# Two grouped-key attention layers and two gMLP layers on one core: normalisation and division moved to GpSimd, score slots of two and two banks in nine groups, a longer ring early, and a new choice of the key tiles that VectorE takes

## The chip, the cores and the metric

The kernel runs on one core of a Trainium2 chip. The core has TensorE (PE, matrix products into PSUM), VectorE (DVE) and ScalarE (ACT), which both read PSUM, GpSimd (POOL), which works on SBUF alone here, and SyncE (SP), from whose queue every DMA of this kernel is issued. The metric is the device time of one execution in microseconds (us), smaller being better. Before the change it is 1592.44 us, the median of three runs (1591.35 to 1594.88).

## The reference, cut to what matters

Four residual blocks follow each other on 2048 tokens of width 512: attention A, gMLP B, A, B, each behind a layer norm. Attention has 32 query heads of width 16 and one key and value head. Weights and tokens are bf16.

```python
def _A_ref(x, wq, wk, wv, wo):
    q = (x @ wq).reshape(B, S, 32, 16).transpose(0, 2, 1, 3)
    k = x @ wk
    v = x @ wv
    scores = jnp.einsum('bhqd,bkd->bhqk', q, k) * 16 ** (-0.5)
    p = softmax(scores)
    o = jnp.einsum('bhqk,bkd->bhqd', p, v)
    return o.transpose(0, 2, 1, 3).reshape(B, S, 512) @ wo

def _B_ref(x, w_in, w_sp, b_sp, w_out):
    z = gelu(x @ w_in)                    # 1792 columns
    z1, z2 = z[..., :896], layernorm(z[..., 896:])
    g = einsum('ts,bsf->btf', w_sp, z2) + b_sp[None, :, None]
    return (z1 * g) @ w_out

x = x + _A_ref(layernorm(x), ...)
x = x + _B_ref(layernorm(x), ...)
# and both once more
```

## The kernel before

**Work of one layer.** The 2048 tokens are 16 tiles of 128. The queries are cut in nine chunks of two tiles (the last two of one), and each chunk with its heads in 32 groups per layer; a group holds 512 query columns for each of four rows of heads. For every group and each of the 16 key tiles PE makes four score blocks of 128x512 (line 897). The exponentials of these 4096 blocks are the bulk of the kernel.

**Two ways for a key tile.** Of most key tiles the four blocks go through `push_unit` and `push_slot`: blocks are put in a row, and taken from it three and two at a time into two slots of PSUM banks, (0,1,2) and (3,4). ACT takes the exponential of a whole slot in one instruction (line 921: 128x1536 or 128x1024) into `P_ring`, which holds 20 blocks, and PE multiplies them with the values, four at a time (line 940), summing in bank 6. The key tiles that `ON_DVE` lists for the group (234 places in all) go through `push_unit_dve`: each of the four blocks goes into a side bank (5 or 7), DVE turns it into an integer that is the bit pattern of an approximate exponential (line 974, one instruction a block), makes two shifted copies of all four (line 983, 128x2048, two instructions), and PE multiplies the three versions with weighted values (line 989). So a unit on DVE is six DVE instructions, and takes four blocks from ACT. The three versions stand in the buffer `big`, of which a ring of six places is used up to group 24 and of five from there.

**End of a group.** DVE copies bank 6 out (line 1051 or 1048), SP issues a DMA transposition (line 1010), DVE takes the reciprocal of the sixteen denominators of each row (line 1017) and multiplies by it (line 1026, two instructions a group, one where the chunk is one tile), into `o_norm`. At the end of a chunk SP transposes its tiles (line 1060), PE multiplies with `wo` (line 693 is the helper of all products that are made in four column strips, line 698 of those made in one), DVE adds to the tokens `X` (line 1074).

**Layer norms.** `ln_tiles` takes statistics on DVE (lines 796, 797), the inverse deviation on GpSimd (lines 784 and 786: an addition, then a power of -0.5), and normalises a tile on DVE (line 801). `norm_z2` does the same for the gMLP's second half (lines 1251 to 1258). The transposed tokens `xnTA` and `xo` come from the normalised ones by DMA (line 810), and at the start of a layer by PE (line 815). On GpSimd there are besides these only the products of line 1364 at the end of a layer, and memsets at the start.

**gMLP.** It is spread over the attention of the same layer: the products with `w_in` behind each chunk (`b_front`), the product with `w_sp` in two stages after tiles 6 and 12 (`mix_stage`, line 1305), the rest when the layer's attention is over (`mix_late`, lines 1359 and 1364), for layer 1 between the two layers and for layer 2 at the end. The GELUs run on ACT (lines 1207, 1230, 1242 and others).

**What sets the order.** Every operation is recorded with the tiles that it reads and writes, an assumed duration and a priority. `_Graph.schedule` then plays the program through by these durations, and writes for each engine a fixed list of instructions, with semaphore waits between engines. Each engine works through its own list in order. PSUM banks are given out in that play: slots by `slots`, the side banks by `side`; where no slot waits, a free slot bank can serve as a side bank. `filler` puts matmuls that compute nothing where PE would be idle too long (lines 716, 719 and 730). `NEAR`, `P_S` (priority of the score blocks for DVE) and `HOLD_DVE` (how long such a block is held back when a slot is due) are numbers of that play.

Of the kernel before, what the change touches and what calls it, by code (L numbers as in the profile page):

```python
# [44 lines left out]
HOLDS = 1.0  # L45

ON_DVE = ((
          (6,10,14), (6,10,14), (6,10,14), (6,10,14), (4,5,6,13), (8,9,12,14), (4,7,9,10,11), (3,6,14),
          (4,7,10,14), (4,6,8,12), (5,8,9,13), (4,6,10,12), (2,5,7,9,10), (2,8,9,11,12), (5,9,13), (3,4,5,9),
          (3,10,11,14), (2,3,5,8,14), (2,4,9,14), (8,9,12,14), (7,11,13), (2,9,13,14), (3,6,10,14), (4,5,7,13),  # L50
          (3,9,12,13), (8,11,14), (10,13), (3,6,7,13), (2,6,14), (2,4,9,14), (6,10,14), (2,4,12)
), (
          (6,10,14), (10,14), (6,10,14), (14,), (6,10,14), (2,10,14), (2,6,10), (10,14), (4,5,12,14),
          (7,8,11,12,13), (4,5,7,14), (3,12,13,14), (4,8,13), (4,6,9,14), (4,5,6,12), (3,5,8,12),
          (2,7,8,11,14), (3,9,10), (3,4,5,6,12), (7,8,9,10,13), (6,8,13,14), (6,7,9,11), (2,3,4,8,11),
          (6,13,14), (2,5,6,11), (5,7,10), (4,5,7,13), (5,11,13), (4,6,12), (2,8,9,12), (4,8,9,10), (2,3,8,10)
))


# [4 lines left out]
SLOTS_STAGE = ((12, 13, 14, 15), (10, 11, 12, 13, 14, 15), (10, 11, 12, 13, 14, 15))  # L64
FRONTS = (((0, 4, None), (4, 2, 0), (6, 2, None), (8, 4, 6), (12, 2, None), (14, 1, 12), (15, 1, 15)), ((0, 4, None), (4, 2, 0), (6, 2, None), (8, 4, 6), (12, 2, None), (14, 1, 12), (15, 1, 15)))
SHORT_RING = (24, 24)
Z2_LATE = (12, 12)

PR_FRONT = (0.5, 3.5)
WARM_US = 3.4  # L70
WARM = 0.52
WARM_END = 0.55
NEAR = 1
LEAD_PR = 4
GELU_PARTS = 1
EAGER = 4
CHAIN_ACT = 1
KEY_PR = {0: 1.2, 2: 1.7, 4: 2.2, 6: 2.4, 8: 2.7, 10: 2.9, 12: 3.2}
KEYS = (((0, 2), (2, 2), (4, 4), (8, 4), (12, 4)), ((0, 2), (2, 2), (4, 4), (8, 4), (12, 4)))
NFIRST = (4, 8)  # L80
# [2 lines left out]
SLOTS_LATE = ((0, 1, 2, 3, 4, 5, 6), (7, 12, 13, 14, 15, 6), (0, 1, 2, 3, 4, 5, 6, 7, 8, 9, 10, 11, 12, 13, 14, 15))  # L83
POOL0 = {0: (), 2: (0, 1, 2, 3, 4, 5, 6), 4: (1, 3, 5)}
POOL1 = (0, 2, 4, 6)
HOLD_DVE = (1.0, 1.0, 0.4, 1.0)
STAY = 0.3
P_S = 0.2
P_R = 0.3
P_A = 4.0  # L90
WARM_OP = 0.217
# [63 lines left out]
class _Graph:  # L155
# [67 lines left out]
    def schedule(self):  # L223
# [27 lines left out]
        warm = WARM  # L251
        slot_ops = [o for o in self.ops if o.task is not None and o.task.slot is not None and o.eng == "pe"]
        slot_at = 0
        slot_due = -1.0

        def push(t, what, x):
# [14 lines left out]
        def met(s, p):  # L271
# [8 lines left out]
            if s.nleft == 0 and (t is None or t.ops[0] is not s):  # L280
                make_ready(s)

        def banks_for(o):

            t = o.task
            if t.slot is not None:
                bs = self.slots[t.slot]
                return bs if all(bank_free[b] for b in bs) else None
            bs = [b for b in self.side if bank_free[b]]
            if not bs and slot_wait == 0:  # L290
                bs = [b for s in self.slots for b in s if bank_free[b]]
            return bs[:1] or None

        def acquire(o, bs):
# [59 lines left out]
        def filler():  # L354


            nonlocal wake
            if self.warm is None or not 0.0 <= self.warm_after.t0 < now - 0.5:
                return None
            while past and past[0][0] < now - WARM_US:  # L360
                past.pop(0)
            have = sum(x for _, x in past)
            if have >= warm * WARM_US:
                drop = next(t for i, (t, _) in enumerate(past)
                            if have - sum(x for _, x in past[:i + 1]) < warm * WARM_US)
                t = max(drop + WARM_US, now) + 0.01
                if wake < now or t < wake:
                    wake = t
                    push(t, 2, None)
                return None  # L370
            if pv_open:
                m = 0 if last_mode == 0 else 2
                o = _Op("pe", lambda e: self.zeros(e, m), WARM_OP, PE_LAT, FILLER, len(self.ops), None, None, m)
                o.deps[self.warm_after] = 1
                self.ops.append(o)
                return o
            bs = [b for b in self.side if bank_free[b]]
            if not bs and slot_wait == 0:
                bs = [b for s in self.slots for b in s if bank_free[b]]
            if pv_empty is not None:  # L380
                bs = [self.pvb]
            if not bs:
                return None
            b = bs[0]
            m = 0 if last_mode == 0 else 2
            o = _Op("pe", lambda e: self.warm(e, b, m), WARM_OP, PE_LAT, FILLER, len(self.ops), None, None, m)
            o.deps[self.warm_after] = 1
            if b == self.pvb:
                o.deps[pv_empty] = 1
                self.ops.append(o)  # L390
                return o
            for q in bank_last[b]:
                o.deps[q] = max(o.deps.get(q, 0), 0 if q.eng == "pe" else 1)
            self.ops.append(o)
            return o
# [153 lines left out]
def bass_interleave_layers__grouped_kv_mqa__mixer_gmlp__prompt_kernel(  # L549
# [17 lines left out]
    QC = 512  # L567
    NQC = S // QC
    CT = QC // P
    G = _Graph(nc, (5, 7), ((0, 1, 2), (3, 4)))  # L570
    op = G.op

    ps_all = G.es.enter_context(nc.psum_tensor("ps_all", [P, 4096], FP32))
# [17 lines left out]
    ident32 = G.sb([P, P], FP32, "ident32")  # L591
    idle = G.sb([P, 1], FP32, "idle")
    mhalf = G.sb([P, 1], FP32, "mhalf")
    X = G.sb([P, NT, D], BF16, "X")

    kT_rep = G.sb([P, 2, S], BF16, "kT_rep")
# [72 lines left out]
    def dve(fn, us, r, w, prio=5):  # L669
        return op("dve", fn, max(us - DVE_LAT, 0.06), r=r, w=w, prio=prio, lat=DVE_LAT)  # L670
# [29 lines left out]
    def side(wide):  # L700
# [5 lines left out]
    op("pool", lambda e: e.affine_select(out=ident[:], in_=ident[:], compare_op=ALU.not_equal, fill=1.0, base=0,  # L706
                                         pattern=[[-1, P]], channel_multiplier=1), 0.3, r=["ident"], w=["ident"])
    op("pool", lambda e: e.memset(mhalf[:], -0.5), 0.1, w=["mhalf"])
    op("pool", lambda e: e.memset(zeros[:], 0.0), 0.2, w=["zeros"])
    G.warm_after = op("pool", lambda e: e.memset(ones[:], 1.0), 0.2, w=["ones"])  # L710
    G.pvb = PVB
# [79 lines left out]
    def ln_tiles(t0, n, xT, keys, per_tile, prio=5):  # L791
# [6 lines left out]
        rstd("1", ve1, rs1, mv1, t0 % CT, n, per_tile, prio)  # L798
        for t in ts:
            i = t % CT  # L800
            dve(lambda e, i=i, t=t: e.tensor_scalar(xn[:, i, :], X[:, t, :], mv1[:, i, 0:1], rs1[:, i:i + 1],
                                                    op0=ALU.subtract, op1=ALU.mult), 0.4,
                [("X", t), ("mv1", i), ("rs1", i)], [("xn", i)], prio)
        t = t0
        while t < t0 + n:
            m = 1 if per_tile else min(2, t0 + n - t)
# [69 lines left out]
        return gi // 2 % NQ, gi % 2  # L876

    main = {"blocks": [], "i": 0, "s": 0, "pv": [], "last": None}
    SLOTS = ((0, 3), (3, 2))

    def push_unit(u):

        main["pv"].append([u, 4])
        for j in range(4):
            main["blocks"].append((u, j))
        while len(main["blocks"]) >= SLOTS[main["i"] % 2][1]:
            push_slot(SLOTS[main["i"] % 2][1])

    def flush_units():
        if main["blocks"]:  # L890
# [9 lines left out]
    def push_slot(n):  # L900
        blocks = main["blocks"][:n]
        del main["blocks"][:n]
        i = main["i"] % 2
        main["i"] += 1
        b0 = SLOTS[i][0]
        s0 = main["s"] % NPR
        main["s"] += SLOTS[i][1]
        tk = _Task(i)

        def pe_s(e):  # L910
# [86 lines left out]
    def finish_group(gi):  # L997
# [15 lines left out]
        def src():  # L1013
            if not isinstance(tk, _Task):
                return ot[:, par, :, :].rearrange("p b (j r) -> p b j r", j=4)
            return bank16(tk.bank)[:, 0:CT * P].rearrange("p (b j r) -> p b j r", b=CT, j=4)
        dve(lambda e: e.reciprocal(rden[:], src()[:, :, :, DH]), 0.26, [tk], ["rden"], pr)
        a = g % 2
        cs = [g // 2 * m + u for u in range(m)]
        if n == 1:  # L1020
# [1 line left out]
        else:  # L1022
            parts = [(u * n, n, o_norm[:, i0:i0 + n, c * P:(c + 1) * P].rearrange(
                "p b (j a d) -> p a b j d", j=4, a=2)[:, a], [c]) for u, c in enumerate(cs)]
        for b0, nb, dst, of in parts:
            dve(lambda e, b0=b0, nb=nb, dst=dst: e.tensor_tensor(
                dst, src()[:, b0:b0 + nb, :, 0:DH], rden[:, b0:b0 + nb, :, None].to_broadcast([P, nb, 4, DH]),
                ALU.mult), 0.15 + 0.07 * nb, [tk, "rden"],
                [("on", c, a, i) for c in of for i in range(i0, i0 + n)], pr)
# [57 lines left out]
    def attn_first(t0, n):  # L1087

        for gi in range(NFIRST[now["layer"]]):
            have = sum(GROUPS[gi][:2])  # L1090
            if have > t0 + n:
                continue
# [16 lines left out]
    def attn_rest():  # L1109
        phr["base"] = 0  # L1110
        for gi in range(NFIRST[now["layer"]], len(GROUPS)):
            now["group"] = gi
            on_dve = ON_DVE[now["layer"]][gi]
            phr["ring"] = NRING if gi < SHORT_RING[now["layer"]] else 5
            for kt in range(NT):
                u = (q_of(gi), kt, kt == 0, kt == NT - 1, lambda gi=gi: group_done(gi, False),
                     kt >= NT - 1 - NEAR)
                if kt in on_dve:
                    push_unit_dve(u)
                else:  # L1120
                    push_unit(u)
# [124 lines left out]
    def norm_z2(t0, n, fine, pr):  # L1246
# [8 lines left out]
        rstd("2", ve2, rs2, mv2, t0 % CT, n, fine, pr)  # L1255
        for t in ts:
            i = t % CT
            dve(lambda e, i=i, t=t: e.tensor_scalar(z2n[:, t, :], z2n[:, t, :], mv2[:, i, 0:1], rs2[:, i:i + 1],
                                                    op0=ALU.subtract, op1=ALU.mult), 0.45,
                Z2(t) + [("mv2", i), ("rs2", i)], Z2(t), pr)  # L1260

    gs = {"n": 0}

# [222 lines left out]
```

## Time and profile before

| | |
|---|---|
| median of three runs | 1592.44 us |
| the profiled execution, its own time | 1594.17 us |
| its span | 1592.4 us |
| granted TensorE clock, mean | 0.995 |
| GpSimd busy | 88.5 us in 138 instructions |
| DMA queues, share of 16 engines | 25.5% |
| first exponential / last exponential of line 921 starts | 15.25 us / about 1514 us |
| tail after attention | 1516 to 1592.4 us, ACT busy 18.9 us of it |

A page of the profile gives busy times of the engines, their busy share in 40 slices of the span, the chain of waits that ended last, and groups of equal instructions with the mean duration of one. Two instructions of one engine can overlap at their ends, so that the distance from one start to the next is less than the duration: two instructions of line 974 of 684 ns each take 1.20 us together. Busy time counts such overlaps once.

### The profile page before, as it was taken

To read this page: it belongs to the slowest core of one execution; us is meant where nothing else is said; L and a number is where in the kernel's file an instruction comes from. 1 tells how busy PE (TensorE), PEld (TensorE's weight loads), DVE (VectorE), ACT (ScalarE), POOL (GpSimd) and SP (SyncE) were. 2 spreads that over 40 slices of the span, in tenths; PEclk is the share of its full clock that TensorE was granted. 3 is DMA by queue.
4 is the path that set the end of the run, shared out by engine and by line. 5 is a ranking of instruction groups with operands and counts; after the bars stand their busy time and mean duration, and the time that the engine had idled before them with its cause. 6 is when DMAs were issued, how large, how long until landed. Compare 5 with 4: busy or idle time off the path is not lost.

```text
span 1592.4 us, 41272 instructions
## 1 busy us (share of the span) xinstructions
PE 1499.7 (94%) x18283; PEld 492.4 (31%) x18311; DVE 1370.3 (86%) x2482; ACT 1501.3 (94%) x1312; POOL 88.5 (6%) x138
## 2 busy tenths in 40 slices
PE   8989899999999999999899989999999999999989
PEld 3222222232333333333422222323223323323344
DVE  7888889999998888896788789999899998988876
ACT  6999999999999999999699999999999999999950
POOL 2000000000000000000311000000000000000033
PEclk8999999999999999999999999999999999999999
DMA  4500010101021342645321021101121114245483
GB/s 104 130 15 11 8 28 8 16 10 41 21 48 51 90 108 68 170 98 157 116 81 34 15 52 34 22 8 19 47 64 28 22 51 107 48 124 134 114 240 131
DMA packets 188562, 106.38 MB, mean 67 GB/s; under 512 B 151264, under 2 KB 160096, under 8 KB 188384
## 3 DMA queue, kind: packets, MB, share of 16 engines
q1 hardware_dynamic: 188384, 103.75, 25.5%
q8 instruction: 143, 2.34, 0.6%
q14 instruction: 35, 0.29, 0.1%
HBM read 36.34 MB, written 31.46 MB: 43 GB/s over the span
## 4 chain that ended last, share of the span: by engine, by line
ACT 76%; PE 17%; DVE 4%; DMA 1%; issue 1%; POOL 0%; SPq 0%; DVEq 0%
ACT P_ring L921 74%; PE ps_all L693 5%; PE ps_all L897 4%; PE ps_all L698 4%; PE ps_all L940 2%; ACT z2n L1207 1%; PE ps_all L989 1%; DVE big L974 0%; DMA gp_scratch<-big 0%; DVE st L796 0%; DVE X L1074 0%; DVE st L1251 0%; DVE big L1359 0%; ACT L921 0%; DMA big<-gp_scratch 0%
## 5 line engine op out<-in xcount | busy, mean ns | idle before, releaser
L921 ACT ACTIVATE P_ring<-ps_all 128x1024 bf16<-128x1024 f32 (+1 forms) x1265 | 1433.6, 1371 | 22.0 <-PE ps_all L897 21.2
L974 DVE TENSOR_SCALAR big<-ps_all 128x512 int16<-128x512 f32 x936 | 617.7, 685 | 108.0 <-PE ps_all L897 102.7
L897 PE MATMUL ps_all<-qT,kT_rep 32*128 32x512 bf16 x4096 | 592.7, 385 | 68.2 <-ACT P_ring L921 51.6
L897 PEld LDWEIGHTS ps_all<-qT,kT_rep 32*128 32x128 bf16 x4096 | 150.3, 91 | 580.8 <-ACT P_ring L921 483.2
L983 DVE TENSOR_SCALAR big<-big 128x2048 int16<-128x2048 int16 x468 | 309.5, 683 | 3.2 <-PE ps_all L989 0.8
L940 PE MATMUL ps_all<-P_ring,V_aug 128*32 128x512 bf16 x3160 | 295.8, 387 | 2.3 <-DVE z2n L1038 0.7
L989 PE MATMUL ps_all<-big,V_ph 128*32 128x512 bf16 x2808 | 241.5, 384 | 2.1 <-DVE big L983 1.3
L940 PEld LDWEIGHTS ps_all<-P_ring,V_aug 128*32 128x32 bf16 x3160 | 75.0, 94 | 152.9 <-issue 130.3
L989 PEld LDWEIGHTS ps_all<-big,V_ph 128*32 128x32 bf16 x2808 | 66.4, 95 | 95.2 <-issue 50.1
L693 PE MATMUL ps_all<-xnTA,z2n 128*32 128x512 bf16 x1344 | 93.9, 381 | 0.0
L784 POOL TENSOR_SCALAR ve<-mv 128x1 f32<-128x1 f32 (+2 forms) x44 | 14.1, 321 | 1423.1 <-DVE mv L797 1194.8
L730 PE MATMUL ps_all<-ones,zeros 128*32 128x512 bf16 x864 | 70.5, 387 | 0.0
L693 PE MATMUL ps_all<-w_in_r,xo 128*32 128x448 bf16 x960 | 61.5, 354 | 0.0
L1074 DVE TENSOR_TENSOR X<-ps_all,X 128x512 bf16<-128x512 f32 x64 | 43.8, 685 | 18.5 <-PE ps_all L698 15.5
L693 PE MATMUL ps_all<-xo,w_in_r 128*32 128x256 bf16 (+1 forms) x1120 | 56.4, 317 | 1.0 <-DVE z1c L1197 0.5
L698 PE MATMUL ps_all<-w_out_r,z1c 128*128 128x512 bf16 x213 | 53.3, 381 | 1.1 <-issue 0.6
L1305 DVE TENSOR_TENSOR big<-ps_all,bsp 128x512 f32<-128x512 f32 x56 | 38.3, 684 | 14.4 <-PE ps_all L693 14.2
L693 PE MATMUL ps_all<-z2n 128*32 128x512 bf16 x672 | 49.1, 382 | 0.2 <-DVE big L974 0.2
L693 PE MATMUL ps_all<-z1c,z2n 128*32 128x512 bf16 x672 | 48.7, 382 | 0.0
L1305 DVE TENSOR_TENSOR big<-ps_all,big 128x512 f32<-128x512 f32 x56 | 37.9, 682 | 11.6 <-PE ps_all L693 11.4
L796 DVE BATCH_NORM_STATS2 st<-X 128x6 f32<-128x512 bf16 x64 | 43.4, 686 | 2.5 <-DMA X<-in_A_x_dram 1.8
L1359 DVE TENSOR_TENSOR big<-ps_all,big 128x512 f32<-128x512 f32 (+1 forms) x56 | 34.7, 647 | 9.5 <-PE ps_all L698 5.3
(96 smaller groups left out, 930.9 us busy)
## 6 DMA issues: line engine op xcount, KB each, us to landing
gp_scratch<-big SPq DMA_DIRECT2D x112, 256.0 KB, 2.2
big<-gp_scratch SPq DMA_DIRECT2D x105, 256.0 KB, 3.0
out_dram<-X SPq DMA_DIRECT2D x16, 128.0 KB, 1.7
w_in_r<-in_B_w_in_dram SPq DMA_DIRECT2D x1, 1792.0 KB, 9.3
big<-gp_scratch SPq DMA_DIRECT2D x14, 128.0 KB, 2.3
X<-in_A_x_dram SPq DMA_DIRECT2D x3, 512.0 KB, 6.5
bsp<-in_B_b_sp_dram SPq DMA_DIRECT2D x8, 128.0 KB, 3.6
ot<-oT SPq DMA_TRANSPOSE x62, 2.4
```

What stands on the lines that cost most here:

```text
L693: ins = e.matmul(out_[32 * j:32 * j + 32, :], lhs[:, 32 * j:32 * j + 32], rhs, tile_position=(0, 32 * j), start=start, stop=stop)
L698: return e.matmul(out_, lhs, rhs, start=start, stop=stop)
L730: ins = e.matmul(bank32(PVB)[32 * j:32 * j + 32, :], zeros[:, 0:32], mv, tile_position=(0, 32 * j), start=False, stop=False)
L796: dve(lambda e, i=i, t=t: e.bn_stats(st1[:, i, :], X[:, t, :]), 0.66, [("X", t)], [("st1", i)], prio)
L897: return e.matmul(out, kT_rep[32 * j:32 * j + 32, a, u[1] * P:(u[1] + 1) * P], qT[32 * j:32 * j + 32, q, :], tile_position=(32 * j, 0), st ...
L921: return e.activation(P_ring[:, s0:s0 + n, :], bank32(b0, n).rearrange("p (k q) -> p k q", k=n), ACTF.Exp, scale=E_SCALE)
L940: ins = e.matmul(bank32(PVB)[32 * j:32 * j + 32, :], V_aug[:, kt, :], P_ring[:, s, :], tile_position=(0, 32 * j), start=first, stop=last)
L974: o = dve(lambda e, box=box, tk=tk: e.tensor_scalar(ph16[:, tiles[0], heads["of"][box[0]] * QC:(heads["of"][box[0]] + 1) * QC], bank32(tk. ...
L983: dve(lambda e, a=a: e.tensor_scalar(ph16[:, tiles[a], :], ph16[:, tiles[0], :], float(PH_A[a]), None, op0=ALU.add), 0.69, base, BIG(tiles ...
L989: ins = e.matmul(bank32(PVB)[32 * j:32 * j + 32, :], V_ph[:, a, kt, :], big[:, tiles[a], j * QC:(j + 1) * QC], tile_position=(0, 32 * j), ...
L1074: dve(lambda e: e.tensor_tensor(X[:, t, :], bank32(tk.bank), X[:, t, :], ALU.add), 0.69, [tk, ("X", t)], [("X", t)], prio)
L1305: dve(lambda e, part=part, tk=tk: e.tensor_tensor(part, bank32(tk.bank), part if st else bsp[:], ALU.add), 0.69, [tk] + ([] if st else ["b ...
```

## The change

1. **GpSimd takes three kinds of DVE work.** `POOL_XN`: the normalising of tokens (line 801), but for the first four tiles of layer 1, for the first chunk of layer 2 and for the last chunk's part of the chain between layers. `POOL_Z2`: that of z2 (line 1258), for 24 of 32 tiles. `POOL_ON`: the division at a group's end, for 62 of 64 groups, where the reciprocal becomes a power of -1 with a tensor of minus ones (`mone`), over 128x16, and the products follow.
2. **Slots.** A third slot, (0,1), is there beside (0,1,2) and (3,4). In nine groups (five of layer 1, four of layer 2, the bits of `NARROW`) the slots alternate (0,1) and (3,4), two blocks each. Bank 2 can then serve as a side bank. The place in `P_ring` starts again at 0 where a slot would not fit.
3. **Ring.** `EARLY_RING`: in the groups below 12 the ring of `big` has eight places.
4. **Places.** `ON_DVE` is another table: 248 places, 128 in layer 1 and 120 in layer 2 (before: 119 and 115). Groups 4 to 7 of layer 1 have 5, 5, 5 and 6 (before: 4, 4, 5 and 3).
5. **Numbers of the order.** `NEAR` 1 to 0, `HOLD_DVE[0]` 1.0 to 0.6, `P_S` 0.2 to 0.6. The lists of all engines are made anew.

```diff
 ON_DVE = ((
-          (6,10,14), (6,10,14), (6,10,14), (6,10,14), (4,5,6,13), (8,9,12,14), (4,7,9,10,11), (3,6,14),
...
+          (6,10,14), (6,10,14), (6,10,14), (6,10,14), (2,4,7,12,14), (2,4,7,8,10), (2,5,9,10,12),
+          (4,5,6,9,10,12), (6,11,12,14), (2,5,10,11,14), (5,10,11,12,13), (7,8,11,13), (4,5,6,10),
...
+EARLY_RING = (12, 12)
-NEAR = 1
+NEAR = 0
+NARROW = (8407808, 84426752)
+POOL_ON = 1
+POOL_XN = 1
+POOL_Z2 = 1
-HOLD_DVE = (1.0, 1.0, 0.4, 1.0)
+HOLD_DVE = (0.6, 1.0, 0.4, 1.0)
-P_S = 0.2
+P_S = 0.6
...
+        def narrow():
+
+            while lead_slots and lead_slots[0] < slot_at:
+                lead_slots.pop(0)
+            return bool(lead_slots) and slot_ops[lead_slots[0]].task.slot == 2
...
             bs = [b for b in self.side if bank_free[b]]
+            if not bs and bank_free[2] and narrow():
+                bs = [2]
...
-    G = _Graph(nc, (5, 7), ((0, 1, 2), (3, 4)))
+    G = _Graph(nc, (5, 7), ((0, 1, 2), (3, 4), (0, 1)))
...
-            dve(lambda e, i=i, t=t: e.tensor_scalar(xn[:, i, :], X[:, t, :], mv1[:, i, 0:1], rs1[:, i:i + 1],
-                                                    op0=ALU.subtract, op1=ALU.mult), 0.4,
-                [("X", t), ("mv1", i), ("rs1", i)], [("xn", i)], prio)
+            on_pool = POOL_XN and not G.chain and (now["layer"] or t0 >= CT or xT is xo)
+            op("pool" if on_pool else "dve", lambda e, i=i, t=t: e.tensor_scalar(
+                xn[:, i, :], X[:, t, :], mv1[:, i, 0:1], rs1[:, i:i + 1], op0=ALU.subtract, op1=ALU.mult),
+               0.9 if on_pool else 0.4 - DVE_LAT, r=[("X", t), ("mv1", i), ("rs1", i)], w=[("xn", i)], prio=prio,
+               lat=0.0 if on_pool else DVE_LAT)
...
-    SLOTS = ((0, 3), (3, 2))
+
+    def next_slot():
+
+        if main["i"] % 2:
+            return 1, 3, 2
+        return (2, 0, 2) if NARROW[now["layer"]] >> now["gi"] & 1 else (0, 0, 3)
...
-        s0 = main["s"] % NPR
-        main["s"] += SLOTS[i][1]
+        if main["s"] + n > NPR:
+            main["s"] = 0
+        s0 = main["s"]
+        main["s"] += n
...
-        dve(lambda e: e.reciprocal(rden[:], src()[:, :, :, DH]), 0.26, [tk], ["rden"], pr)
+        on_pool = POOL_ON and not G.chain
+        if on_pool:
+            op("pool", lambda e: e.tensor_tensor(rden[:], src()[:, :, :, DH], mone[:, :, None].to_broadcast([P, CT, 4]),
+                                                 ALU.pow), 0.9, r=[tk, "mone"], w=["rden"], prio=pr)
+        else:
+            dve(lambda e: e.reciprocal(rden[:], src()[:, :, :, DH]), 0.26, [tk], ["rden"], pr)
...
+            if on_pool:
+                op("pool", lambda e, b0=b0, nb=nb, dst=dst: e.tensor_tensor(
+                    dst, src()[:, b0:b0 + nb, :, 0:DH], rden[:, b0:b0 + nb, :, None].to_broadcast([P, nb, 4, DH]),
+                    ALU.mult), 0.25 + 0.14 * nb, r=[tk, "rden"], w=[("on", c, a, i) for c in of for i in range(i0, i0 + n)],
+                   prio=pr)
+                continue
...
-            phr["ring"] = NRING if gi < SHORT_RING[now["layer"]] else 5
+            phr["ring"] = 8 if gi < EARLY_RING[now["layer"]] else NRING if gi < SHORT_RING[now["layer"]] else 5
...
-            dve(lambda e, i=i, t=t: e.tensor_scalar(z2n[:, t, :], z2n[:, t, :], mv2[:, i, 0:1], rs2[:, i:i + 1],
-                                                    op0=ALU.subtract, op1=ALU.mult), 0.45,
-                Z2(t) + [("mv2", i), ("rs2", i)], Z2(t), pr)
+            on_pool = POOL_Z2 and not fine and pr != 0.6
+            op("pool" if on_pool else "dve", lambda e, i=i, t=t: e.tensor_scalar(
+                z2n[:, t, :], z2n[:, t, :], mv2[:, i, 0:1], rs2[:, i:i + 1], op0=ALU.subtract, op1=ALU.mult),
+               1.5 if on_pool else 0.45 - DVE_LAT, r=Z2(t) + [("mv2", i), ("rs2", i)], w=Z2(t), prio=pr,
+               lat=0.0 if on_pool else DVE_LAT)
```

The instructions of the two built programs differ by these counts:

| engine | instruction | before | after |
|---|---|---|---|
| ACT | exponential 128x1536 (line 921) | 631 | 534 |
| ACT | exponential 128x1024 (line 921) | 633 | 751 |
| ACT | exponential 128x512 (line 921) | 1 | 0 |
| DVE | line 974, 128x512 | 936 | 992 |
| DVE | line 983, 128x2048 | 468 | 496 |
| DVE, then GpSimd | reciprocal / power 128x16 | 62 | 62 |
| DVE, then GpSimd | division, 128x128 / 128x256 | 112 / 6 | 112 / 6 |
| DVE, then GpSimd | tokens normalised, 128x512 | 64 on DVE | 8 on DVE, 56 on GpSimd |
| DVE, then GpSimd | z2 normalised, 128x896 | 32 on DVE | 8 on DVE, 24 on GpSimd |
| PE | line 940 / line 989 | 3160 / 2808 | 3104 / 2976 |
| PE | fillers (lines 716, 719, 730) | 1243 | 853 |

## The prediction

> **What bounds the kernel now.** I read the page's busy times and slices first, then the chain of waits, then the groups by form, then the waits of DVE, and last single stretches of the timeline.
>
> ```profile
> PE 1499.7 (94%) x18283; PEld 492.4 (31%) x18311; DVE 1370.3 (86%) x2482; ACT 1501.3 (94%) x1312; POOL 88.5 (6%) x138
> DVE  7888889999998888896788789999899998988876
> ACT  6999999999999999999699999999999999999950
> ```
>
> ACT is at nine tenths or more in 36 of 40 slices; it is short of work only at the start, between the layers and in the tail. PE's 94% hold 1243 fillers, so PE has room. The chain of waits (first its shares, then single pieces: start us, us, what) says the same:
>
> ```profile
> ACT 76%; PE 17%; DVE 4%; DMA 1%; issue 1%; POOL 0%; SPq 0%; DVEq 0%
> 51.88 291.64 ACT P_ring L921 x258
> 1375.66 1.20 DVE big L974 x2
> 1378.58 1.20 DVE big L983 x2
> ```
>
> In the first long piece 258 exponentials, 129 of each width, follow each other in 291.64 us: 2.26 us a pair of five blocks. The two last lines give DVE's real price: 0.60 us from start to start where the duration is 0.684, that is 0.084 less. The groups by form (mean ns after the comma):
>
> ```profile
> L921 ACT ACTIVATE P_ring<-ps_all 128x1536 bf16<-128x1536 f32 x631 | 998.9, 1583 | 7.5 <-PE ps_all L897 6.7
> L921 ACT ACTIVATE P_ring<-ps_all 128x1024 bf16<-128x1024 f32 x633 | 735.2, 1162 | 14.5 <-PE ps_all L897 14.5
> ```
>
> A block more is 1583 - 1162 = 421 ns. With 2.26 us for five blocks in two instructions, what an instruction costs by itself is (2.26 - 5 x 0.421) / 2 = 0.08 us. In 1592.4 us these instructions wait 22.0 us in all: ACT is packed, and the time falls by what its queue loses, as long as it stays packed.
>
> **ACT's queue.** 14 units move to DVE: 56 blocks x 0.421 = -23.6 us. The program has 1285 exponentials in place of 1265, since the nine narrow groups cut finer: 20 x 0.08 = +1.6. Sum **-22.0 us**. The GELUs on ACT are the same.
>
> **DVE's queue.** Added: 56 of line 974 and 28 of line 983, 84 x 0.60 = +50.4 us. Removed, each at its mean less 0.084, from these rows:
>
> ```profile
> L974 DVE TENSOR_SCALAR big<-ps_all 128x512 int16<-128x512 f32 x936 | 617.7, 685 | 108.0 <-PE ps_all L897 102.7
> L983 DVE TENSOR_SCALAR big<-big 128x2048 int16<-128x2048 int16 x468 | 309.5, 683 | 3.2 <-PE ps_all L989 0.8
> L1026 DVE TENSOR_TENSOR o_norm<-ot,rden 128x128 bf16<-128x128 bf16 x112 | 28.8, 284 | 0.4
> L801 DVE TENSOR_SCALAR xn<-X,mv,rs 128x512 bf16<-128x512 bf16 x64 | 26.9, 448 | 6.9 <-POOL rs L786 6.7
> L1017 DVE RECIPROCAL rden<-ot 128x16 f32<-128x16 bf16 x62 | 15.1, 244 | 0.2 <-DMA ot<-oT 0.2
> L1258 DVE TENSOR_SCALAR z2n<-z2n,mv,rs 128x896 bf16<-128x896 bf16 x32 | 14.9, 502 | 1.9 <-POOL rs L786 1.9
> ```
>
> 62 x 0.160 + 112 x 0.200 + 6 x 0.334 (the 128x256 form, 418 ns) + 56 x 0.364 + 24 x 0.418 = 9.9 + 22.4 + 2.0 + 20.4 + 10.0 = -64.7 us. Net -14 us: DVE as a whole gets a little lighter, and its 102.7 us of waiting for score blocks show that it has room on average. But not everywhere: counting instructions between the ends of groups in the built order, and pricing them as above, groups 5 to 9 of layer 1 have 97 us of ACT and 96 us of DVE work (before: 107 and 85). Nearly half of ACT's gain lies there, with DVE at 99%. Elsewhere DVE is near 0.89 of ACT.
>
> **GpSimd's queue.** Nothing in the trace shows these operations at these sizes. The nearest rows:
>
> ```profile
> L1364 POOL TENSOR_TENSOR z1c<-big,z1c 128x512 bf16<-128x512 f32 x25 | 32.7, 1318 | 59.7 <-DVE big L1359 59.7
> L786 POOL TENSOR_TENSOR rs<-ve,mhalf 128x4 f32<-128x4 f32 x14 | 14.7, 1049 | 1.2
> L786 POOL TENSOR_TENSOR rs<-ve,mhalf 128x1 f32<-128x1 f32 x20 | 11.6, 578 | 1.7
> L1364 POOL TENSOR_TENSOR z1c<-big,z1c 128x256 bf16<-128x256 f32 x7 | 4.5, 672 | 4.2 <-DVE big L1359 4.2
> ```
>
> The power: 0.157 us a column from 1 to 4 columns, so 16 columns are 0.578 + 15 x 0.157 = 2.93 us; the low end is 0.58 (no more than one column). I take 2.93. The division: 2.52 ns a column from 256 to 512, so 0.35 us for 128, 0.67 at the high end. Tokens, one tensor input: between 0.53 (the memset of 128x512, 527 ns) and 1.32; I take 0.9. z2, 896 columns: 0.8 (from the 128x1536 memset, 1379 ns) to 2.3; I take 1.5. Sum 62 x 2.93 + 112 x 0.35 + 6 x 0.67 + 56 x 0.9 + 24 x 1.5 = 182 + 39 + 4 + 50 + 36 = 311 us (low 120, high 390), on an engine that is busy 88.5 us. It has room; what counts is who waits for it. Behind a late power stand the two divisions, then at a chunk's end SP's transposition and PE's product with `wo`. In the built order the first such product stands at least 13.4 us of ACT work behind the last value product of the chunk. The chain needs 0.69 (line 1051) + 2.4 (DMA to landing) + 2.93 + 2 x 0.35 + 2 x 0.68 (each division once behind a line 983) + 1.24 (SP's first issue) + 2.5 (landing) = 11.8 us. It is covered, by 1.6 us. The normalised tokens: first `w_in` product at least 8.1 us behind the last PE result that its chain needs (before: 6.7), which covers the +0.5 us of the slower tile. SP's next transposition (line 1010) newly waits for GpSimd's division of two groups earlier, some 40 us before: nothing. DVE's statistics of line 797 and 1253 newly wait for GpSimd's normalising of the tile that used the place before, tens of us earlier: nothing. These cost nothing on my sum; without the cover, rival 2.
>
> **GpSimd against DVE.** The timeline shows what a neighbour costs (POOL and DVE lines of two stretches):
>
> ```profile
> 787.60 1.16 POOL L1364 TENSOR_TENSOR z1c<-big,z1c 128x512 bf16<-128x512 f32 x1
> 787.66 1.24 DVE L801 TENSOR_SCALAR xn<-X,mv,rs 128x512 bf16<-128x512 bf16 x1 [0.43 <-POOL rs L786]
> ```
> ```profile
> 1000.94 1.09 POOL L786 TENSOR_TENSOR rs<-ve,mhalf 128x4 f32<-128x4 f32 x1
> 1001.32 0.68 DVE L983 TENSOR_SCALAR big<-big 128x2048 int16<-128x2048 int16 x1
> ```
>
> The SBUF-to-SBUF instruction of DVE that starts behind GpSimd's product lasts 1.24 us, until 0.14 us after the product's end, where one without a neighbour takes 0.41 us. Line 983 beside the power keeps its 0.68. So I count GpSimd's products and normalisings as blocking (130 us of the 311), not its powers. Line 983 starts 496 times; 130 of some 1580 us is 8%, so 41 of them wait, for half of a GpSimd operation and the tail, 0.4 us: 16 us of DVE time, 0.25 us a group. Lines that read PSUM kept 0.68 beside GpSimd throughout. What of it reaches ACT: in groups 5 to 9 all of it, 1.3 us, and since DVE there has no room for any wait for a score block, some 4% of 96 us more, 4 us; in the other groups, with 2 us of room each, a fifth of the rest, 3 us. Sum **+8 us** (bounds: 0, if ACT stays as packed as now; 40, if half a microsecond a group and the early groups run at DVE's 10% idle of now).
>
> The Trainium skill (SBUF — State Buffer, Who interferes with whom) says that DVE's two-port instructions and any GpSimd operation exclude each other for the whole instruction, whoever is second. By that rule the powers would block too, which is rival 3; the row at 1001.32 disagrees, for a power of four columns.
>
> **The rest.** The longer ring frees line 983's next unit earlier in groups 4 to 11 and is what lets five units stand in a group; its places 6 and 7 are next written by line 1305, which starts after group 11: no wait. The restart of `P_ring` leaves a place or two unused at a wrap, of 20. PE: 112 value products more, 390 fillers fewer: hidden, as fillers are what is left over; if the clock fell for want of them, PEclk would leave 9. Start, layer boundary and tail: the first chunk of layer 2 keeps DVE, later chunks normalise on GpSimd behind its own line 1364 products, where DVE already waited for those (787.66). 0 us, bounds -2 and +4.
>
> **Sum.** -22 + 8 = -14: the span goes from 1592.4 to 1578.4, the profiled execution's 1594.17 to 1580.2. The median shown is 1.7 under that execution, so the forecast is **1578 us**.
>
> **Rivals.** (1) *ACT stays as packed as now*: -22, 1570 us. For it: 22.0 us of idle on line 921 in the whole run. Against it: groups 5 to 9. (2) *GpSimd is late at the ends of chunks and PE waits in order*: 16 ends at 0.5 to 1 us are 8 to 16 us on top, 1586 to 1594 us. For it: only 1.6 us of cover. Against it: DMA slack is often larger than the least. (3) *The power holds DVE off as well*: 311 us of GpSimd time block; 496 x 311/1580 = 98 starts of line 983 wait, 1.05 us on average (half of 2.93 for most), 103 us of DVE in place of 16, 1.6 us a group, of which the room of 2 us swallows half: 1578 + 43 = 1621 us, slower. It decides from 0.34 us a group (22/64) that reaches ACT. For it: xn beside line 1364; against it: three line 983 beside powers, all at 0.68 to 0.70. (4) *It does nothing*: another engine sets ACT's pace, 1592 us; against it the packed queue.
>
> **Chances.** Forecast 0.52 (its own range 1572 to 1586), rival 1 0.17, rival 2 0.15, rival 3 and milder forms of it 0.13, rival 4 0.03. A measurement here can tell about 0.2%, 3.2 us, from no change. Faster by more than that: 0.52 + 0.17 + half of rival 2 = 0.77; within: 0.06; slower: 0.17. The range 1567 to 1598 takes in rivals 1, 2 and 4, and leaves out 2 in 10.
>
> **What would show it.** Line 921: 534 and 751 instructions, its idle still under 35 us; a pair of narrow slots 2 x 0.92 us. Line 983's mean 0.70 to 0.72, not over 0.75. The power near 2.9 us. The idle of line 897 behind DVE lines up by a few us, most before 220 us. ACT's slices 9 as before. I am wrong if ACT's idle grows by more than 20 us, or if PE's waits for `wo` products show GpSimd behind them.

## The result, and the profile after

The changed kernel takes 1634.16 us (median of four runs, 1630.43 to 1634.77) against 1591.89 us before: ratio 1.0258 [1.0237, 1.0279]. By the ratio it is 41 us slower (the medians lie 42 us apart), where 14 us faster was forecast. The profiled execution took 1630.43 us; its span is 1628.5 us. Line numbers have moved: the exponential is line 946 now (921 before), scores 921 (897), products in strips 709 (693), DVE's copies 1008 (983), DVE's integers 999 (974), the value products 965 (940) and 1014 (989), other products 714 (698), the stages of `w_sp` 1344 (1305), tokens 819 (801), z2 1296 (1258), the aggregates of their statistics 814 (797) and 1290 (1253); the power and the divisions on GpSimd are 1044 and 1057, its products at a layer's end 1403 (1364).

The page after: busy times, ACT's busy share and the granted clock in 40 slices, and the shares of the chain of waits.

```profile
PE 1526.4 (94%) x18033; PEld 491.4 (30%) x18033; DVE 1373.7 (84%) x2306; ACT 1484.0 (91%) x1332; POOL 541.4 (33%) x399
...
ACT  5999999989999997999699899999799999969960
...
PEclk9999999989999998999999999999799999979999
...
ACT 60%; PE 21%; POOL 9%; DVE 6%; issue 2%; DMA 1%; SPq 0%; POOLq 0%; DVEq 0%
```

ACT lost its packed row: slices 8, 15, 28 and 35 (counted from 0) fall to 7 or 8, or to 6 in slice 35, and in the same slices the clock is below 9 (slice 22 falls to 8 with the clock at 9). GpSimd is on the chain for 9% of the span, where it had 0%. The groups of ACT and GpSimd by form (busy us, mean ns of one, idle before):

```profile
L946 ACT ACTIVATE P_ring<-ps_all 128x1536 bf16<-128x1536 f32 x534 | 830.2, 1555 | 44.1 <-PE ps_all L921 43.3
L946 ACT ACTIVATE P_ring<-ps_all 128x1024 bf16<-128x1024 f32 x751 | 806.8, 1128 | 36.0 <-PE ps_all L921 35.5
L1044 POOL TENSOR_TENSOR rden<-ot,mone 128x16 f32<-128x16 bf16 x62 | 187.6, 3026 | 697.5 <-DMA ot<-oT 697.3
L819 POOL TENSOR_SCALAR xn<-X,mv,rs 128x512 bf16<-128x512 bf16 x56 | 127.5, 2286 | 1.8
L1296 POOL TENSOR_SCALAR z2n<-z2n,mv,rs 128x896 bf16<-128x896 bf16 x24 | 85.4, 3569 | 0.7
```

In front of the exponentials ACT idles 80.1 us where it idled 22.0, nearly all of it for scores. On the page their busy time is 1416.3 us, 17.3 less than before: so -17 + 58 = +41 us on this line, more than the 36 us by which the span grew. The normalisings on GpSimd take 2.29 us a tile of tokens and 3.57 us a tile of z2; the plan assumes 0.9 and 1.5. Who waits for them (the waits of PE, then of DVE: us, times, longest):

```profile
PE ps_all L921 <- ACT P_ring L946: 31.8, 110, 1.0
PE ps_all L709 <- POOL z2n L1296: 15.9, 5, 7.0
PE ps_all L921 <- DVE big L999: 6.5, 19, 2.2
PE ps_all L1014 <- DVE big L1008: 5.6, 4, 3.4
```
```profile
DVE mv L1290 <- POOL z2n L1296: 12.5, 6, 3.6
DVE mv L814 <- POOL xn L819: 11.3, 8, 1.9
```

None of these waits on GpSimd is in the profile before. The worst place, first GpSimd and PE on the timeline, then the same stretch by windows (its length, the busy time of PE, PEld, DVE, ACT and POOL with the number of instructions, the clock, then DMA):

```profile
629.49 14.72 POOL L1296 TENSOR_SCALAR z2n<-z2n,mv,rs 128x896 bf16<-128x896 bf16 x4
...
644.26 1.05 PE L709 MATMUL ps_all<-xnTA,z2n 128*32 128x512 bf16 x8 [7.00 <-POOL z2n L1296]
```
```profile
627.00:637.00 10.00, 7.68 (x83) 2.17 (x83) 9.49 (x15) 9.12 (x8) 9.66 (x5) 1.00 0.01 2
637.00:644.00 7.00, 0.26 (x8) 0.00 (x0) 0.73 (x2) 0.14 (x1) 7.00 (x2) 0.62 0.00 0
644.00:651.00 7.00, 6.74 (x68) 1.74 (x68) 3.27 (x5) 3.86 (x4) 0.21 (x1) 0.65 0.20 59
651.00:660.00 9.00, 9.00 (x130) 2.71 (x122) 6.83 (x11) 9.00 (x9) 3.69 (x3) 1.00 0.49 142
```

PE stands in front of a `w_sp` product whose z2 tile is not there. Everything behind it on PE's list waits, the score blocks for ACT too: in these 7 us ACT is busy 0.14 us and DVE 0.73. Then the clock is at 0.65 for 7 us more and ACT gets half its work, with PE busy 6.74 of 7.00 us. So one late batch is followed by two losses: the wait, and a stretch of slow clock behind it. Over the whole run, counted record by record between the first and the last exponential, ACT idles 78.4 us where it idled 20.9. Of these 57.5 us more, 20 fall where PE stands still, 28 where PE is busy at a clock of 0.5, and 10 where PE is busy at the full clock. This says when ACT idled, not what the slow clock alone costs.

### The profile page after: what moved, and what is told of

Same layout as the page of the kernel before. It is cut to its first block, busy times and chain, and to the rows that moved or that the text cites. A ratio compares the mean times of both kernels' runs of the same rounds, so it can differ in the third digit from the quotient of the medians.

```text
span 1628.5 us, 40947 instructions
## 1 busy us (share of the span) xinstructions
PE 1526.4 (94%) x18033; PEld 491.4 (30%) x18033; DVE 1373.7 (84%) x2306; ACT 1484.0 (91%) x1332; POOL 541.4 (33%) x399
## 4 chain that ended last, share of the span: by engine, by line
ACT 60%; PE 21%; POOL 9%; DVE 6%; issue 2%; DMA 1%; SPq 0%; POOLq 0%; DVEq 0%
ACT P_ring L946 59%; PE ps_all L709 6%; PE ps_all L921 6%; POOL z2n L1296 5%; PE ps_all L714 4%; PE ps_all L965 3%; PE ps_all L1014 2%; POOL xn L819 2%; DVE big L999 1%; POOL rs L803 1%; ACT z2n L1244 1%; DVE st L813 1%; POOL rden L1044 1%; DVE st L1288 1%; DVE big L1008 0%
## 5 line engine op out<-in xcount | busy, mean ns | idle before, releaser
L946 ACT ACTIVATE P_ring<-ps_all 128x1024 bf16<-128x1024 f32 (+1 forms) x1285 | 1416.3, 1305 | 80.1 <-PE ps_all L921 78.8
L999 DVE TENSOR_SCALAR big<-ps_all 128x512 int16<-128x512 f32 x992 | 653.4, 685 | 102.9 <-PE ps_all L921 97.6
L921 PE MATMUL ps_all<-qT,kT_rep 32*128 32x512 bf16 x4096 | 615.7, 391 | 51.1 <-ACT P_ring L946 31.8
L1044 POOL TENSOR_TENSOR rden<-ot,mone 128x16 f32<-128x16 bf16 x62 | 187.6, 3026 | 697.5 <-DMA ot<-oT 697.3
L1008 DVE TENSOR_SCALAR big<-big 128x2048 int16<-128x2048 int16 x496 | 341.3, 707 | 6.0 <-PE ps_all L1014 2.7
L921 PEld LDWEIGHTS ps_all<-qT,kT_rep 32*128 32x128 bf16 x4096 | 155.9, 91 | 584.4 <-ACT P_ring L946 446.1
L1014 PE MATMUL ps_all<-big,V_ph 128*32 128x512 bf16 x2976 | 263.1, 390 | 6.4 <-DVE big L1008 5.6
L819 POOL TENSOR_SCALAR xn<-X,mv,rs 128x512 bf16<-128x512 bf16 x56 | 127.5, 2286 | 1.8
L1296 POOL TENSOR_SCALAR z2n<-z2n,mv,rs 128x896 bf16<-128x896 bf16 x24 | 85.4, 3569 | 0.7
L1057 POOL TENSOR_TENSOR o_norm<-ot,rden 128x128 bf16<-128x128 bf16 (+1 forms) x118 | 52.3, 463 | 4.7
```

The lines of the kernel that those rows point to most:

```text
L819: op("pool" if on_pool else "dve", lambda e, i=i, t=t: e.tensor_scalar(xn[:, i, :], X[:, t, :], mv1[:, i, 0:1], rs1[:, i:i + 1], op0=ALU.s ...
L921: return e.matmul(out, kT_rep[32 * j:32 * j + 32, a, u[1] * P:(u[1] + 1) * P], qT[32 * j:32 * j + 32, q, :], tile_position=(32 * j, 0), st ...
L946: return e.activation(P_ring[:, s0:s0 + n, :], bank32(b0, n).rearrange("p (k q) -> p k q", k=n), ACTF.Exp, scale=E_SCALE)
L999: o = dve(lambda e, box=box, tk=tk: e.tensor_scalar(ph16[:, tiles[0], heads["of"][box[0]] * QC:(heads["of"][box[0]] + 1) * QC], bank32(tk. ...
L1008: dve(lambda e, a=a: e.tensor_scalar(ph16[:, tiles[a], :], ph16[:, tiles[0], :], float(PH_A[a]), None, op0=ALU.add), 0.69, base, BIG(tiles ...
L1014: ins = e.matmul(bank32(PVB)[32 * j:32 * j + 32, :], V_ph[:, a, kt, :], big[:, tiles[a], j * QC:(j + 1) * QC], tile_position=(0, 32 * j), ...
```

## The experiments

**1. Is it the lateness of z2?** All lists stay as in the changed kernel; GpSimd's piece is cut until it lasts about as long as the plan assumes (340 of 896 columns, where the operation is on GpSimd).

```diff
-                z2n[:, t, :], z2n[:, t, :], mv2[:, i, 0:1], ...
+                z2n[:, t, 0:340] if on_pool else z2n[:, t, :], z2n[:, t, 0:340] if on_pool else z2n[:, t, :], ...
```

> The changed kernel with every engine's list unchanged, but GpSimd's normalising of z2 (line 1296) works on 340 of the 896 columns: 0.37 + 340 x 3.3 ns = 1.5 us, which is what the plan assumes, in place of 3.35 us. The other 556 columns stay as they are. Theory A (GpSimd is late against the plan: z2 arrives 7 us after PE's place for it, PE waits in order, its clock falls to 0.5 and ACT starves): the four places at 351, 637, 1143 and 1425 us lose their 48 us, time 1634 - 45 = 1589 us, clock 0.99. Theory B (DVE is held off at the shared port and is too full in groups 5 to 9): only the 6 us that z2 adds to line 1008 go, 1626 us. Theory C (390 fillers fewer let the clock fall by themselves): 1634 us, clock 0.97.

1593.60 us, ratio 1.0013 [0.9996, 1.0030]. 39 us of the 41 are gone with one operation's duration, at 1.72 us a tile. That is 5 us from theory A's number, while B's 1626 and C's 1634 are far off. A's clock was not reached: 0.98 to 0.99 in the ten runs, and the places where tokens are late still show a fallen clock.

**2. The tokens too, and the power too.** The first line is z2_xn_short's, on top of z2_short (160 of 512 columns, on GpSimd alone); the second is all_short's, on top of both (3 of the 16 results). What is cut away, here and in z2_short, isn't computed.

```diff
+                xn[:, i, 0:160] if on_pool else xn[:, i, :], X[:, t, 0:160] if on_pool else X[:, t, :], ...
...
+            op("pool", lambda e: e.tensor_tensor(rden[:, 0:1, 0:3], src()[:, 0:1, 0:3, DH], ...
```

> As z2_short, and GpSimd's normalising of tokens (line 819) works on 160 of 512 columns: 0.9 us, as planned, in place of 2.07 us. The other columns keep old values. Theory A: also the losses at 235, 929 and at the start go, 10 to 15 us more than z2_short: 1577 us, which is the forecast of the prediction. Theory B: 1622 us. Theory C: 1634 us.

> As z2_xn_short (every engine's list unchanged, z2 normalised on 340 of 896 columns, tokens on 160 of 512), and the power of -1 (line 1044) on 3 of 16 columns: 0.42 + 3 x 0.157 = 0.9 us, as the plan assumes, in place of 3.03 us. The other denominators are left at 1 or at old values. If the power's 2.1 us of lateness is covered, as the prediction has it: the time of z2_xn_short, 1575 us, within 3 us. If the divisions too are waited for: 1565 us or less.

z2_xn_short: 1575.32 us, 0.9895 [0.9879, 0.9911]: 19 us more where A had 10 to 15, and 2 us from A's time. all_short: 1566.57 us, 0.9846 [0.9832, 0.9861]: 8 us more, so the power's lateness was not covered. All three together: some 66 us (1.0258 - 0.9846 = 0.0412 of 1591).

Where the power costs its 8 us can be seen in z2_xn_short. Nearly all of ACT's idle time that all_short doesn't have lies from 1106 to 1126 us (the last line is a window):

```profile
1098.96 2.93 POOL L1044 TENSOR_TENSOR rden<-ot,mone 128x16 f32<-128x16 bf16 x1
...
1105.96 0.21 DVE L1290 BATCH_NORM_AGGREGATE mv<-st 128x2 f32<-128x12 f32 x1 [1.79 <-POOL z2n L1296]
...
1106.78 0.40 PE L1014 MATMUL ps_all<-big,V_ph 128*32 128x512 bf16 x4 [1.54 <-DVE big L1008]
...
1110.00:1118.00 8.00, 8.00 (x55) 1.31 (x51) 5.49 (x9) 5.91 (x6) 5.53 (x5) 0.50 0.01 2
```

The power stands in GpSimd's queue in front of a normalising of z2, DVE's statistics wait for that one, line 1008 comes late behind them, PE waits 1.54 us, and then the clock is at 0.5. PE's waits for the division's own result sum to 0.7 us in the whole run.

The exponentials of all_short, by form:

```profile
L947 ACT ACTIVATE P_ring<-ps_all 128x1536 bf16<-128x1536 f32 x534 | 837.4, 1568 | 8.6 <-PE ps_all L922 8.1
L947 ACT ACTIVATE P_ring<-ps_all 128x1024 bf16<-128x1024 f32 x751 | 812.6, 1145 | 14.0 <-PE ps_all L922 13.9
```

22.6 us of idle, before it was 22.0: where GpSimd's durations are those of the plan, ACT is packed as well as it was, at 248 places and with the narrow slots. The clock is 0.997.

**3. The work back on DVE, all lists made anew** (POOL_Z2 = 0; then POOL_XN = 0 as well).

> The changed kernel with POOL_Z2 = 0: z2 is normalised on DVE (24 x 0.42 = 10 us more there), all lists made anew. Theory A: what is left is the tokens' lateness, 1634 - 45 + 0 to 5 = 1590 us. Theory B: DVE gets fuller, 1634 us or more.

> The changed kernel with POOL_Z2 = 0 and POOL_XN = 0: GpSimd keeps the division at a group's end alone, whose power takes 3.03 us where the plan has 0.9. Theory A: no place left where z2 or tokens are late, 1575 to 1580 us, clock 0.99; the power's 2.1 us of lateness is covered. Theory B: 28 us more on DVE than with all three on GpSimd, over 1620 us.

1636.38 us, 1.0274 [1.0247, 1.0302], and 1621.18 us, 1.0186 [1.0169, 1.0203]. Both expectations of A failed, though PE's waits on line 1296 are down to 0.3 us in z2_dve and gone in z2_xn_dve. Both times are those that theory B gave (1634 or more, over 1620), so this pair by itself speaks for B; what speaks against it are the runs above, which left the lists alone, and experiments 4 and 5. The waits of ACT in z2_xn_dve:

```profile
ACT P_ring L946 <- PE ps_all L921: 54.5, 43, 12.0
```

The lists differ, and so do the places where ACT starves; in all_short the same line has 22.0 us. The kind of loss differs too: of the 58.5 us that ACT idles in z2_xn_dve between its first and last exponential, 53 fall where PE is busy at the full clock (26 of 78.4 in the changed kernel). That the table of places belongs to one plan is the likely reading, and not shown by this pair: the power still lasts longer than its plan says.

**4. The plan told the truth.**

```diff
-               0.9 if on_pool else 0.4 - DVE_LAT, ...
+               2.25 if on_pool else 0.4 - DVE_LAT, ...
-               1.5 if on_pool else 0.45 - DVE_LAT, ...
+               3.55 if on_pool else 0.45 - DVE_LAT, ...
-                                                 ALU.pow), 0.9, ...
+                                                 ALU.pow), 3.0, ...
-                    ALU.mult), 0.25 + 0.14 * nb, ...
+                    ALU.mult), 0.29 + 0.085 * nb, ...
```

> The changed kernel, where the plan is told the durations that GpSimd has in the profile after: 2.25 us for tokens, 3.55 for z2, 3.0 for the power, 0.46 and 0.63 for the divisions. All lists are made anew, the 248 places stay. Theory A: no PE wait on line 1296 and a clock of 0.99, but the places were found for the other lists, so ACT idles in new spots as in z2_xn_dve: 1605 to 1625 us. If places do not matter: 1577 us. Theory B: 1630 us, as the work on GpSimd is the same.

1607.12 us, 1.0098 [1.0081, 1.0115], clock 0.996: 27 us better than the changed kernel with the same instructions in another order, and still slower than before, as expected of places that were found for other lists. Theory B had 1630 us here, as GpSimd's work is the same.

**5. The shared port by itself.** First, 138 added instructions:

```diff
+        if not G.chain and g < 2 * n - 1:
+            for _ in range(3):
+                op("pool", lambda e: e.tensor_scalar(dump[:], dump[:], mhalf[:, 0:1], mhalf[:, 0:1], op0=ALU.subtract,
+                                                     op1=ALU.mult), 0.0, r=[("oT", par)], w=["dump"], prio=9)
```

> The kernel before, with the lists of PE, DVE, ACT and SP unchanged, and 138 instructions added on GpSimd that no engine waits for: at the end of each group that does not end a chunk three normalisings of a scratch tile of 128x896, 3.35 us each, 462 us in all. So GpSimd is as busy as in the changed kernel (541 us) and holds the shared port, but nothing is late. Theory A (lateness against the plan is the cause, the port costs little): from the changed kernel, where line 1008 lost 4.6 us beside 85 us of z2, line 983 loses some 25 us of DVE time, of which a fifth reaches ACT: 1597 us, no more than 1602. Theory B (the port is the cause): over 1612 us.

1684.72 us, 1.0590 [1.0556, 1.0623], far over A's 1602 and inside B's "over 1612". But it doesn't measure the port alone: the added work stood on GpSimd in front of work that DVE waits for (waits of DVE):

```profile
DVE z2n L1265 <- POOL rs L788: 21.8, 6, 7.8
DVE xn L803 <- POOL rs L788: 21.5, 14, 7.6
DVE oT L1055 <- POOL dump L1017: 19.9, 5, 6.2
```

So it is one more case of lateness: 63 us of DVE waits in a list that nobody planned for them are in the 94 us that it lost; how the rest divides between the port and a mean clock of 0.968 it doesn't show. Then, without that fault, 75 instructions behind `rden` in groups where GpSimd is otherwise idle:

> The port alone, mended: the kernel before with the lists of PE, DVE, ACT and SP unchanged, and 75 GpSimd instructions that no engine has to wait for, five normalisings of a scratch tile of 128x896 (16.8 us) in each of 15 groups in which GpSimd has no other work (in before_busy the added work stood in front of the inverse deviations and of the copies out of bank 6, so DVE waited for GpSimd, 63 us). 251 us of port time. Theory A: line 983 loses 251 x 0.05 = 13 us of DVE time, ACT at most half of it, 1591 to 1598 us. Theory B: in the changed kernel 350 us of port time would have cost 67 us, so here 48 us, 1638 us.

1599.38 us, 1.0065 [1.0043, 1.0087]. DVE's copies by form, and the waits of ACT:

```profile
L985 DVE TENSOR_SCALAR big<-big 128x2048 int16<-128x2048 int16 x468 | 328.6, 724 | 3.2 <-PE ps_all L991 0.8
```
```profile
ACT P_ring L923 <- PE ps_all L899: 24.2, 26, 11.8
```

The mean goes from 683 to 724 ns, 19 us of DVE over 468 instructions, and 8 to 10 us reach the time, at a clock of 0.999. That is 1 us over A's range and 39 us under B's 1638: the port is real, and about a fifth of what theory B needed.

**6. All the work, in the changed kernel's lists.** GpSimd keeps what fits the plan's duration, DVE does the rest beside it in instructions that the plan gives no time (the last line is in split only; in split_zx the power stays whole on GpSimd):

```diff
+                rest = op("dve", lambda e, i=i, t=t: e.tensor_scalar(
+                    z2n[:, t, 340:FH], z2n[:, t, 340:FH], mv2[:, i, 0:1], rs2[:, i:i + 1], ...), 0.0, ...)
...
+                op("dve", lambda e, i=i, t=t: e.tensor_scalar(xn[:, i, 160:D], X[:, t, 160:D], ...), 0.0, ...)
...
+            op("dve", lambda e: e.reciprocal(rden[:, 1:CT, :], src()[:, 1:CT, :, DH]), 0.0, ...)
```

> The whole computation, with the lists of PE, ACT and SP of the changed kernel: GpSimd does only as much of each operation as fits the duration that the plan assumes (z2: 340 of 896 columns, tokens: 160 of 512, the power: 4 of 16), and DVE does the rest in instructions that take no time in the plan. DVE gets 24 of some 0.35 us, 56 of 0.25 us and 62 of 0.15 us, 32 us in all, of the 200 us that it idles in all_short. Theory A (late against the plan): all_short's 1567 us, plus a third of those 32 us: 1577 us, 0.9% faster than before. Theory B' (DVE is so full with 248 places that it is the bound as soon as it keeps its old work): 1567 + 32 = 1599 us or more, slower than before.

> As split, but the power stays on GpSimd as a whole (3.03 us). The power's share is then 9 us, by all_short against z2_xn_short, less the 9 us of DVE that it spares: 1575 + a third of 23 us = 1582 us. Slower than split: the power belongs on DVE; faster: on GpSimd.

1601.94 us, 1.0063 [1.0047, 1.0079], and 1609.40 us, 1.0105 [1.0091, 1.0119]: split is at B', and the power is better off on DVE; split_zx is 27 us over its expected 1582. By their pages DVE is busy 33 us more in split than in all_short (1397.8 against 1364.5), and this unplanned work costs 35 us. Where, by windows of split:

```profile
602.00:608.00 6.00, 4.48 (x48) 0.93 (x46) 5.86 (x11) 5.99 (x6) 0.00 (x0) 0.85 0.01 3
608.00:614.00 6.00, 6.00 (x44) 1.12 (x44) 4.59 (x12) 4.15 (x5) 3.94 (x4) 0.50 0.00 0
614.00:620.00 6.00, 6.00 (x48) 1.13 (x40) 3.99 (x10) 4.62 (x4) 2.89 (x3) 0.52 0.00 0
```

DVE is full (5.86 of 6), PE idles 1.5 us, the clock falls to 0.5, and then PE is busy throughout while ACT has a quarter of its time free.

**7. Does the clock make it dear?** Each filler of PE in split made twice as long.

```diff
-            ins = e.matmul(bank32(PVB)[32 * j:32 * j + 32, :], zeros[:, 0:32], mv, ...)
+            for _ in range(2):
+                ins = e.matmul(bank32(PVB)[32 * j:32 * j + 32, :], zeros[:, 0:32], mv, ...)
```

> split with every filler of PE (lines 719 and 730 of the kernel before, four matmuls of zeros or ones) made of eight matmuls, the plan and all other instructions unchanged: 550 matmuls more, some 28 us of PE in all, where PE idles anyway. In split PE's granted clock falls to 0.5 for 61 us in all (mean 0.981), at 340 to 357, 606 to 633, 907 and 1408 us, and ACT loses most there. If the fallen clock is what makes delays of 1 to 2 us dear: clock 0.99 or more, 1602 - 25 = 1577 us. If the delays by themselves are the price: 1602 us or, with PE's longer fillers in the way of score blocks, up to 1615 us.

1612.81 us, 1.0125 [1.0106, 1.0145], clock 0.986 after 0.981. The stretches of slow clock sum to 44 us after 61, and yet it is slower: ACT's idle time where PE is busy at the full clock rose from 28 to 42 us. So longer fillers cost PE's time elsewhere, and this doesn't tell the two apart: what part of split's loss is the slow clock and what part the delay stays open.

**8. A plan with true durations and its own places.** Only the division on GpSimd, measured durations, places on DVE and six numbers of the order found anew (the places and the numbers are not shown).

```diff
-POOL_XN = 1
-POOL_Z2 = 1
+POOL_XN = 0
+POOL_Z2 = 0
...
-                                                 ALU.pow), 0.9, ...
+                                                 ALU.pow), 3.0, ...
...
```

> The changed kernel where GpSimd keeps only the division at a group's end (POOL_XN = POOL_Z2 = 0), the plan has its measured durations (power 3.0 us, divisions 0.46 and 0.63), and the places on DVE and six numbers of the order (P_S 0.2, P_R 0.4, STAY 0.2, P_A 4.5, HOLD_DVE 0.6 and 1.2 in its first two entries) were found anew for that plan; the narrow groups stay. 1289 exponentials in 3108 blocks: ACT's queue is 52 x 0.421 - 24 x 0.08 = 20 us shorter than before. Theory A (a plan whose durations are true is kept): ACT stays nearly as packed as in z2_xn_dve is not, at the level of before and all_short, and the time is 1591 - 20 + 5 to 15 for DVE's fuller groups: 1576 to 1586 us, clock 0.99. If 248 places and narrow slots are too much for DVE whatever the plan: 1600 us or more.

1589.36 us, 0.9987 [0.9978, 0.9996] over 11 runs: it beats both kernels, the one before by 2 us. The expected 1576 to 1586 was missed: the exponentials wait 35.5 us for scores, 14 more than before. z2_xn_dve, with the same work on GpSimd, the old places and numbers and the power planned at 0.9 us, was 32 us slower; which of the three brings how much isn't shown.

## Why the prediction was wrong, step by step

- **ACT's queue, -22 us: right.** all_short has the changed kernel's lists; on its page the exponentials are busy 1411.5 us against 1433.6, 22.1 less, and it takes 24 us less than before (1566.57 against 1590.39).
- **DVE at 99% in groups 5 to 9: no harm in itself.** In all_short these groups run from 141 to about 243 us, and of these 102.00 us ACT is busy 102.00, with DVE at 98.89. In split, with DVE's added work, ACT loses 1.8 us there; most of its loss stands at 340 to 358, 610 to 634 and near 910 and 1410 us.
- **The step that failed: "Tokens, one tensor input: between 0.53 ... and 1.32; I take 0.9. z2, 896 columns: 0.8 ... to 2.3; I take 1.5."** Measured 2.29 and 3.57 us, over both high ends; the shortest are 2.07 and 3.35. I took one tensor input for cheaper than two, and so came to the very values that the plan assumes, which hid that anything would be late. But this form with two scalars per partition has its own price: by the shortest, 3.3 ns a column from 512 to 896, where the product of line 1403 has 1.9 from 256 to 512 (0.67 and 1.15 us). No row before had the form at a size that shows it: line 784 has one to four columns. The honest bounds were wider than memset and product. The Trainium skill (GPSIMD Engine Reference, Engine selection) calls one-input elementwise work on GpSimd roughly line rate; by its clock of 1.2 GHz that is an estimate of 0.43 us for 512 columns, and this trace disagrees by five times.
- **"It is covered ... These cost nothing on my sum": wrong for all three.** For z2 I worked out no cover at all: four tiles stand one behind the other in front of a stage of `w_sp`, 14.7 us in place of 6.0 at the place shown. Taken away in this order, z2 cost 39 us, tokens 19, the power 8. The power's duration was right (2.93 against 3.03), but its cover was worked out for its own chain to `wo` alone. What it made late was the normalising behind it in GpSimd's queue, as z2_xn_short shows at 1099 us.
- **"DVE's statistics newly wait for GpSimd's normalising of the tile that used the place before, tens of us earlier: nothing": wrong.** The next batch of statistics comes right behind; lines 1290 and 814 waited 23.8 us.
- **Rival 2 had the kind of wait right, and the place and the price wrong.** GpSimd was late and PE waited in order, but for z2 in front of `w_sp` products, not at the ends of chunks: of my two signs of being wrong, ACT's idle time grew by 58 us, while `wo` products show no GpSimd behind them. In place of "0.5 to 1 us" at 16 places it was up to 7 us at few, with a slow clock behind them.
- **The port, +8 us: right in size.** Line 1008's mean is 707 ns, 12 us over 496 instructions; before_quiet shows 8 to 10 us for a like load. Rival 3 is false: the 65 of line 1008 that started while a power ran in this trace had a mean of 0.688 us.
- **"If the clock fell for want of fillers": it fell for another reason,** PE standing still in front of a wait, which fillers can't fill since they stand behind it on its list. all_short has the same 853 fillers and a clock of 0.997.

## What to carry to other kernels

In a kernel whose order is fixed beforehand from assumed durations, an engine that is idle on the page is not free: a piece of work that lasts longer than assumed stops every in-order list that has its result next, and the fully packed engine pays. Price an operation that the trace doesn't show from a row of the same form, with the same kinds of operands, or bound it from a row known to be dearer; and compare new durations with the plan's before anything else. A table tuned against one plan can lose in another more than it brought (1607 and 1621 us here): where undoing a part of a tuned change makes all lists anew, the result holds the loss of the tuning as well. Keep the lists, and change one duration.

## What the hardware showed beyond that

- Short standstills of PE were enough for a fall of the granted clock to 0.5. In the changed kernel it fell during or within 2 us of waits of 1.6 to 7.0 us, in split behind one of 1.0 us (603 us). Not every one of that length did it: behind 1.6 us at 1113 us in the kernel before, the clock stayed. And in all_short it fell for 3.4 us at 1054 us, where PE had idled 0.5 us of the 6.8 before. The stretches at 0.5 lasted 3.4 to 17.1 us, some 89 us in all in the changed kernel (mean 0.973), before 17 us (0.995).
- The Trainium skill (SBUF — State Buffer, Who interferes with whom) has the second of two contenders for the shared port blocked for the whole instruction. Here a normalising of z2 began at 633.24 us and took 3.35 us; line 1008 at 633.50 was held until about 0.95 us after that start, and the next one, at 634.79, ran its usual 0.68 us while GpSimd was still at work. Of the 21 of line 1008 that started while a z2 tile was being normalised, the four at 1.5 to 2.2 us into it ran 0.68 us, three at 0.2 to 0.3 us took 1.36 to 1.41, and all seven at 2.7 to 3.0 us took 1.04 to 1.41. So in this trace such an operation held DVE off near its beginning and near its end, not throughout.
